# Queries' high parts, the place of a low part, and the first pair's loads in an attention with experts

## The chip, the cores and the metric

The kernel runs on one core of a Trainium2 chip, with TensorE (PE), VectorE (DVE), ScalarE (ACT), GpSimd (POOL) and SyncE (SP), which here only issues DMAs. The metric is the device time of one execution in microseconds.

## The reference

```python
q_pool = q.reshape(4, 8, 576, 2, 64).mean(axis=3)           # q, k, v: (4, 8, 1152, 64)
scores = np.matmul(q_pool, k.transpose(0, 1, 3, 2)) / 8     # 576 x 1152 per head
attn = softmax(scores)                                      # row maximum subtracted
x = np.matmul(attn, v) -> (2304, 512)
# each of the 2304 tokens goes to the expert of its largest logit (x @ w_gate, 8 experts)
x[mask_e] = gate * (np.maximum(x[mask_e] @ w1[e], 0) @ w2[e])   # 512 -> 1024 -> 512
out = ((x @ w_a) * (x @ w_b)) @ w_out                           # 512 -> 1536 -> 512
```

## The kernel before

All large products use two float16 parts of each operand: a high part, written by ScalarE, and a low part, the remainder, by VectorE (`scalar_tensor_tensor`: scaled source minus high part) or GpSimd. The work has three stages: the attention (to about 550 us), the experts over slots of 64 tokens, and the last two products.

The attention goes over 16 pairs of heads, `p` = 0 to 15, each in 21 units `u` (`n` = 21 p + u). The program's order is written by hand, and each engine executes its instructions in that order. In unit `n` the loop emits, in this order: the groups `a_units` that are due, the scores of unit `n + 1`, loads and preparation of later pairs (`load`, `prep_k`, `prep_q` and so on, at the units in the table `U`), `norm`, `turn`, `turn_low` and `logits` for the pair before, `p_low` of unit `n - 1` and the product with the values `av` of unit `n - 4`.

- `load(p)` brings raw queries (`qr`, two loads for each head) and keys (`kr`) by five DMAs on SP.
- `prep_q` adds neighbouring queries (GpSimd; VectorE for pair 0) and ScalarE writes the high part `qn[:, :, 0, :]`. `prep_q_low` copies it on VectorE to `qn[:, :, 1, :]` and writes the low part `qln`. `trans_q1` turns both by DMA transposes on SP into `qq` and `qlt`; `trans_k` does so for the keys (`kst`). `spread` copies the last tile of each.
- `a_units` are one or two PE groups of scores in high precision, into a slot of the PSUM pool `ps_a` (tile `sa`, two slots); VectorE reduces each to row maxima `mx`. `finish_max` makes a correction from them that goes through the transposition `rl` (SP) into the scores' second product. The list `a_ends` says by which unit how many groups have been emitted.
- `scores` go to two PSUM slots (`sp`); ScalarE reads each twice (`pt` in float32, `ph` in float16). `p_low` (`pl`) is GpSimd's, and `av` uses `ph` and `pl`.
- `turn(p - 1)` transposes finished outputs on PE into a slot of the same pool `sa` (tile `tp`), ScalarE writes the high part `axh`, and `turn_low` the low part `axl` on VectorE, which is the slot's last reader. Tiles 0 to 3 are turned in unit 7 and their low part comes in unit 9; tile 4 in units 10 and 11. `U["ql"]` puts `prep_q_low(p + 2)` into unit 9 as well, and ahead of `turn_low`.

```python
ps_a = ...tile_pool(name="ps_a", bufs=BA // 2, space=PSUM)      # BA = 4
U = dict(v=[12, 15], vl=[14, 19], kl1=[0, 1], ql1=1, load=12, k=[0, 2], kl=[1, 3], q=6, ql=9,
         n0=13, n1=4, nt=6, t=[7, 10], tl=[9, 11], lg=13, sx=17, g=15, lr=18, lv=1, kc=2, mg=12)
```

Ahead of the loop pair 0 is loaded and prepared at once, with PE kept busy by products of ones (`keep_warm`), the first 15 of pair 0's 27 groups of maxima follow, and `load(1)`, `load_v(0)`, `load(2)` stand on SP behind pair 0's transposes. Behind the loop the last pair's outputs are normalised, turned and routed (`scales`, `gate`, `route`), each in small steps that `aside` takes from the list `gates`.

Of the kernel before, what the change touches and what calls it, by code (L numbers as in the profile page):

```python
# [10 lines left out]
F32 = mybir.dt.float32  # L11
# [16 lines left out]
def attn_moe_kernel(  # L28
# [221 lines left out]
    def bh(p):  # L250
        return p // HP, 2 * (p % HP)

    def load(p):
        b, h = bh(p)
        s = st[p] = {}
        s["kr"] = er2.tile([128, 2, NC, D], F32, tag="kr", name=f"kr{p}")
        s["qr"] = er2.tile([128, 9, 2 * D], F32, tag="qr", name=f"qr{p}")
        for j in range(2):
            nc.sync.dma_start(
                out=s["qr"][:, 4 * j : 4 * j + 4],  # L260
                in_=q[b, h + j, 0:1024].rearrange("(i p r) d -> p i (r d)", p=128, r=2),
            )
            nc.sync.dma_start(
                out=s["qr"][64 * j : 64 * j + 64, 8],
                in_=q[b, h + j, 1024:1152].rearrange("(p r) d -> p (r d)", r=2),
            )
        nc.sync.dma_start(out=s["kr"], in_=k[b, h : h + 2].rearrange("h (p c) d -> p h c d", c=NC))
# [31 lines left out]
    def prep_q(p, eng=nc.gpsimd):  # L299
        s = st[p]  # L300
        qs = s["qs"] = er.tile([128, 9, D], F32, tag="qs", name=f"qs{p}")
        qn = s["qn"] = er2.tile([128, 9, 2, D], F16, tag="qn", name=f"qn{p}")
        eng.tensor_tensor(out=qs, in0=s["qr"][:, :, 0:D], in1=s["qr"][:, :, D:], op=ALU.add)
        nc.scalar.activation(qn[:, :, 0, :], qs, AF.Copy, scale=SC)

    def prep_q_low(p):
        qs, qn = st[p]["qs"], st[p]["qn"]
        nc.vector.tensor_copy(qn[:, :, 1, :], qn[:, :, 0, :])
        nc.vector.scalar_tensor_tensor(
            out=qlnb[p % 3][:, :, 0:D], in0=qs, scalar=SC, in1=qn[:, :, 0, :], op0=ALU.mult, op1=ALU.subtract  # L310
        )
# [15 lines left out]
    def trans_q1(p):  # L327
        s = st[p]
        qq = s["qq"] = qqb[p % 3]
        trans(qq[:, 0 : 9 * 128], s["qn"].rearrange("p t r d -> p (t r d)"))  # L330
        qlt = s["qlt"] = qltb[p % 2]
        trans(qlt[:, 0 : 9 * 128], qlnb[p % 3].rearrange("p t c -> p (t c)"))
# [546 lines left out]
    with tc.manual_schedule():  # L879
        A_0 = 3  # L880
        load(0)
# [10 lines left out]

        keep_warm(37)
        prep_q(0, nc.vector)
        for j in range(2):
            prep_k(0, j)
        prep_q_low(0)
        trans_q1(0)
        spread(0)
        for j in range(2):  # L900
            prep_k_low(0, j)
            trans_k(0, slice(j, j + 1))
        for i in range(3):
            nc.gpsimd.memset(k2b[i][64:66], MC)
        load(1)
        load_v(0)
        load(2)
# [16 lines left out]
        for j in range(2):  # L924
            prep_v(0, j)
            prep_v_low(0, j)
        keep_warm(6)

        def twos(p, ones):
# [5 lines left out]
            (NU * p - 5, 15 - A_0 + 27 * p) for p in range(3, NPAIR)  # L935
# [19 lines left out]
        def l_eng(n):  # L955
# [5 lines left out]
            v=[12, 15], vl=[14, 19], kl1=[0, 1], ql1=1, load=12, k=[0, 2], kl=[1, 3], q=6, ql=9,  # L961
# [3 lines left out]
        for n in range(NPAIR * NU):  # L965
# [10 lines left out]
            if a_due(n + 1) < a_due(n) + 2 and n + 1 < NPAIR * NU:  # L976
                scores(n + 1)
            if u == (U["lv"] if p else 5) and nxt:
                load_v(p + 1)
# [21 lines left out]
            if n in U["kl1"]:  # L1001
                prep_k_low(1, U["kl1"].index(n))
            if n == U["ql1"]:
                trans_k(1)
                prep_q_low(1)
                trans_q1(1)
# [4 lines left out]
            v_ = u if p else u - 2  # L1011
# [21 lines left out]
            if p:  # L1033
                if u == U["n1"]:
                    norm(p - 1, 1)
                if u == U["nt"]:
                    norm_tail(p - 1)
                ut, utl, ulg = [(U["t"], U["tl"], U["lg"]), ([7, 13], [9, 14], 15)][not nxt]
                if u in ut:
                    turn(p - 1, [0, 1, 2, 3] if u == ut[0] else [4])  # L1040
                if u in utl:
                    turn_low(p - 1)
                if u == (U["mg"] if nxt else 15):
                    mag_x(p - 1)
                if u == ulg:
                    logits(p - 1)
                if p % HP == HP - 1 and u == U["sx"]:
                    store_x(p // HP, 0, HP - 1)
                if p % HP == 0 and u == U["g"]:
                    gates.extend(x(p // HP - 1) for x in (scales, gate))  # L1050
# [31 lines left out]
        mag_x(NPAIR - 1)  # L1082
        turn(NPAIR - 1, [0, 1, 2, 3])
        gates.append(scales(B - 1))
        while gates:
            aside()
        split_low(0, 8)
        turn_low(NPAIR - 1)
        split_low(0, 9)
# [3 lines left out]
        gates.append(gate(B - 1))  # L1093
        while gates:
            aside()
        routing = route()
        next(routing)
        for _ in routing:
            pass
# [389 lines left out]
```

## Time and profile before

| | us |
|---|---|
| three runs: median (lowest to highest) | 1289.35 (1283.31 to 1292.65) |
| profiled execution: its own time | 1293.19 |
| its span, first to last instruction | 1291.5 |
| PE busy in the span | 1176.2 |
| mean granted clock of PE, share of full speed | 0.971 |

The span and the rows come from the profiled execution alone. A number in brackets behind a row of a timeline is the idle time of the engine just before, with what ended it. PE's clock has two levels, 1.2 and 2.4 GHz; 1.00 in a window is all of it at 2.4. A PE at the lower level counts as just as busy.

### The profile page before, as it was taken

What the parts mean: (1) busy time and instruction counts of PE and PEld (TensorE: products, weight loads), DVE (VectorE), ACT (ScalarE), POOL (GpSimd) and SP (SyncE); (2) the same over time, 40 slices, a digit from 0 to 9 for tenths busy, and PEclk for the clock granted to TensorE, in tenths of its full rate; (3) what the DMA queues carried; (4) which work ended last, traced back from release to release, by engine and by line L of the source; (5) the groups of instructions that cost most, each with busy time, mean ns of one, the idle gap of its engine ahead of it and who ended that gap; (6) DMA issues with size and microseconds to landing.
All of it is one profiled execution on the core that took longest, in us unless ns stands there. A gap on an engine that the chain in (4) does not pass through costs nothing. (4 is left out here: it accounts for less than half of the span.)

```text
span 1291.5 us, 41065 instructions
## 1 busy us (share of the span) xinstructions
PE 1176.2 (91%) x17154; PEld 819.1 (63%) x17154; DVE 790.5 (61%) x1453; ACT 649.9 (50%) x1325; POOL 538.0 (42%) x504
## 2 busy tenths in 40 slices
PE   7899999999899998579979998989999999999996
PEld 6566665666566656479868997965555555555553
DVE  5878789788877886854485547248677722222221
ACT  4578787788778778532473326225433311111110
POOL 4789888788788888613244322100000000000000
PEclk9999999999999999779999998999999999999998
DMA  6766675565555533153286227013222000000000
GB/s 174 157 118 150 149 183 146 114 147 132 112 111 141 122 76 133 48 200 127 79 319 234 88 80 279 25 37 114 77 87 95 21 1 1 25 25 25 25 21 29
DMA packets 170507, 136.45 MB, mean 106 GB/s; under 512 B 101072, under 2 KB 136400, under 8 KB 170256
## 3 DMA queue, kind: packets, MB, share of 16 engines
q1 hardware_dynamic: 167056, 122.74, 35.5%
q0 software_dynamic: 3200, 10.53, 2.5%
q8 instruction: 136, 2.23, 0.7%
q14 instruction: 115, 0.94, 0.2%
HBM read 94.96 MB, written 9.74 MB: 81 GB/s over the span
## 5 line engine op out<-in xcount | busy, mean ns | idle before, releaser
L430 POOL TENSOR_TENSOR pl<-pt,ph 128x512 f16<-128x512 f32 (+1 forms) x330 | 388.6, 1197 | 92.3 <-ACT ph L412 70.6
L361 DVE TENSOR_REDUCE mx<-sa 128x2 f32<-128x768 f32 x224 | 206.0, 923 | 78.8 <-PE sa L356 76.3
L1399 PEld LDWEIGHTS <-wc 128*128 128x128 f16 x1728 | 169.5, 98 | 124.6 <-PEq L1361 4.4
L410 ACT ACTIVATE pt<-sp 128x512 f32<-128x512 f32 (+1 forms) x336 | 197.5, 588 | 96.3 <-PE sp L403 88.6
L1399 PE MATMUL ab<-x2h,wc 128*128 128x384 f16 x1152 | 211.8, 327 | 4.3 <-DVEq L1361 4.3
L1438 POOL DMA_INDIRECT out_dram<-ob,idxo x18 | 17.7, 982 | 442.3 <-DVE ob L1437 408.9
L452 PEld LDWEIGHTS <-ph 128*128 128x128 f16 (+1 forms) x2880 | 152.3, 101 | 74.3 <-issue 33.7
L412 ACT ACTIVATE ph<-sp 128x512 f16<-128x512 f32 (+1 forms) x331 | 194.8, 589 | 0.0
L356 PE MATMUL sa<-kst,qq 128*128 128x384 f16 x480 | 158.5, 331 | 12.4 <-DVE mx L361 9.8
L452 PE MATMUL av<-vv,ph 128*128 128x65 f16 (+2 forms) x2880 | 169.3, 196 | 0.0
L356 PE MATMUL sa<-kst,qlt 128*128 128x384 f16 x480 | 158.0, 330 | 0.0
L1409 DVE TENSOR_TENSOR gf<-ab,sa 128x384 f32<-128x384 f32 x72 | 40.1, 557 | 192.5 <-PE ab L1399 192.5
L452 PE MATMUL av<-vv,pl 128*128 128x65 f16 (+1 forms) x1440 | 157.0, 195 | 0.0
L403 PE MATMUL sp<-rl,k2b 66*128 66x512 f16 (+1 forms) x576 | 136.0, 290 | 10.3 <-DMA rl<-qln 9.8
L1188 PEld LDWEIGHTS <-w2c 128*128 128x128 f16 x3840 | 126.4, 101 | 29.0 <-issue 20.8
L400 PE MATMUL sp<-qq,kst 128*128 128x512 f16 (+1 forms) x576 | 135.2, 289 | 2.0 <-ACT ph L412 1.8
L1167 PE MATMUL hp<-xh,w1c 128*128 128x64 f16 x2560 | 124.0, 193 | 4.8 <-ACTq L1314 0.9
L1167 PEld LDWEIGHTS <-w1c 128*128 128x128 f16 x3840 | 118.7, 98 | 9.7 <-DVE w1c L871 5.8
L452 PEld LDWEIGHTS <-pl 128*128 128x128 f16 (+1 forms) x1440 | 124.3, 102 | 0.0
L1167 PE MATMUL hp<-xl,w1c 128*128 128x64 f16 x1280 | 119.9, 193 | 0.0
L1188 PE MATMUL yp<-hh,w2c 128*128 128x64 f16 x2560 | 112.4, 198 | 8.0 <-issue 2.9
L1399 PE MATMUL ab<-x2l,wc 128*128 128x384 f16 x576 | 117.8, 327 | 0.0
(228 smaller groups left out, 1817.0 us busy)
## 6 DMA issues: line engine op xcount, KB each, us to landing
raw<-in_moe_w_dram SPq DMA_DIRECT2D x20, 1024.0 KB, 6.5
rbw<-in_moe_w_dram SPq DMA_DIRECT2D x20, 1024.0 KB, 7.1
kr<-in_k_dram SPq DMA_DIRECT2D x16, 576.0 KB, 5.1
vr<-in_v_dram SPq DMA_DIRECT2D x16, 576.0 KB, 5.3
qr<-in_q_dram SPq DMA_DIRECT2D x32, 256.0 KB, 3.6
cl<-in_moe_w_a_dram SPq DMA_DIRECT2D x12, 512.0 KB, 3.5
cl<-in_moe_w_b_dram SPq DMA_DIRECT2D x12, 512.0 KB, 3.5
cl<-in_moe_w_out_dram SPq DMA_DIRECT2D x12, 512.0 KB, 3.5
```

Of the source, the lines that this page charges most:

```text
L356: nc.tensor.matmul(sa[:, i, :KA], lhsT=x[:, 128 * b_ : 128 * b_ + 128], rhs=kst[:, j, ks], start=o == 0, stop=o == len(ops) - 1,)
L361: nc.vector.tensor_reduce(out=s["mx"].rearrange("p t n -> p (t n)")[:, ones[0] : ones[0] + m].rearrange("p (m o) -> p m o", o=1), in_=sa[: ...
L400: nc.tensor.matmul(sp[:, o : o + w], lhsT=s["kst"][:, j, ks], rhs=s["qq"][:, c0 : c0 + w], start=True, stop=False)
L403: nc.tensor.matmul(sp[:, o : o + w], lhsT=k2b[p % 3][:, j, ks], rhs=s["rl", j if w > 64 else 1][0:66, c0 : c0 + w], start=False, stop=True,)
L410: nc.scalar.activation(pt[:, :o], sp[:, :o], AF.Exp, scale=1.0 / (16.0 * SC * SC))
L412: nc.scalar.activation(phb[n % NPB][0][:, :o], sp[:, :o], AF.Exp, scale=1.0 / (16.0 * SC * SC))
L430: eng.tensor_tensor(out=l[:, :w], in0=pts.pop(n)[:, :w], in1=h[:, :w], op=ALU.subtract)
L452: nc.tensor.matmul(o, lhsT=a, rhs=b_, start=first, stop=False, skip_group_check=True)
L1167: nc.tensor.matmul(hp[:, j], lhsT=wc[:, t, i], rhs=g[x][:, i, w], start=first, stop=(j == 3 and i == KD - 1 and x == "xl"), skip_group_che ...
L1188: nc.tensor.matmul(y[:, d], lhsT=wc[:, t, 128 * d : 128 * d + 128], rhs=hs[s, n][x][:, j], start=first, stop=(n == 1 and len(terms) == 1 a ...
L1399: nc.tensor.matmul(ps[:, 0:TB], lhsT=w_[:, t, m, 128 * i : 128 * i + 128], rhs=x_[:, i, ts_], start=(i + j == 0), stop=(j == 2 and i == KD ...
L1409: nc.vector.tensor_tensor(out=gf, in0=pair[1], in1=sa, op=ALU.mult)
```

## The change

In the attention only:

- ScalarE writes the queries' high part to both places of `qn` in one instruction, from a source read twice; VectorE's copy goes. `prep_q`, `prep_q_low` and `trans_q1` take a range of tiles.
- `turn_low` is emitted right behind the scores, ahead of the unit's other work, instead of near its end.
- `a_ends` has the maxima from pair 3 on end one unit sooner (`NU * p - 6`).
- Pair 0's loads are split between SP's and ScalarE's queues, with pair 1's keys on ScalarE's behind head 1's queries. Pair 0's preparation goes tiles 0 to 3, head 0's keys, then tiles 4 to 8, head 1's keys, each with its transposes at once. Five products of ones fewer.
- Pair 1's low parts and transposes go from units 0 and 1 to a place ahead of the loop; `load(2)` goes behind them, on ScalarE's queue. Pair 2's preparation and pair 3's loads come two units later in pair 0 (`u - 4`).
- Behind the loop: `mag_x` and `scales` come behind `turn_low`, `scales` between steps of `gate`, and `split_low(0, 9)` behind the first part of `route`.

```diff
-    def load(p):
+    def load_q(p, j, eng=nc.sync):
+    def load_k(p, eng=nc.sync):
+    def load(p, eng=nc.sync):
...
-    def prep_q(p, eng=nc.gpsimd):
+    def prep_q(p, eng=nc.gpsimd, ts=slice(0, 9)):
...
-        nc.scalar.activation(qn[:, :, 0, :], qs, AF.Copy, scale=SC)
+        qb = qs.rearrange("p t (r d) -> p t r d", r=1).to_broadcast([128, n, 2, D])
+        nc.scalar.activation(qn, qb, AF.Copy, scale=SC)
...
-        nc.vector.tensor_copy(qn[:, :, 1, :], qn[:, :, 0, :])
...
-        load(0)
+        load_q(0, 0)
+        load_q(0, 1, nc.scalar)
+        load_k(0)
+        load_k(1, nc.scalar)
...
-        keep_warm(37)
-        prep_q(0, nc.vector)
-        for j in range(2):
+        keep_warm(32)
+
+        for j, ts in enumerate((slice(0, 4), slice(4, 9))):
+            prep_q(0, nc.vector, ts)
             prep_k(0, j)
-        prep_q_low(0)
-        trans_q1(0)
-        spread(0)
-        for j in range(2):
+            prep_q_low(0, ts)
+            trans_q1(0, ts)
             prep_k_low(0, j)
             trans_k(0, slice(j, j + 1))
+        spread(0)
...
-        load(1)
+        for j in range(2):
+            load_q(1, j)
         load_v(0)
-        load(2)
...
         for j in range(2):
+            prep_k_low(1, j)
+        prep_q_low(1)
+        load(2, nc.scalar)
+        for j in range(2):
             prep_v(0, j)
             prep_v_low(0, j)
+        trans_k(1)
+        trans_q1(1)
         keep_warm(6)
...
-            (NU * p - 5, 15 - A_0 + 27 * p) for p in range(3, NPAIR)
+            (NU * p - 6, 15 - A_0 + 27 * p) for p in range(3, NPAIR)
...
+            ut, utl, ulg = [(U["t"], U["tl"], U["lg"]), ([7, 13], [9, 14], 15)][not nxt]
+            if p and u in utl:
+                turn_low(p - 1)
             if u == (U["lv"] if p else 5) and nxt:
                 load_v(p + 1)
...
-            if n in U["kl1"]:
-                prep_k_low(1, U["kl1"].index(n))
-            if n == U["ql1"]:
-                trans_k(1)
-                prep_q_low(1)
-                trans_q1(1)
...
-            v_ = u if p else u - 2
+            v_ = u if p else u - 4
...
-                if u in utl:
-                    turn_low(p - 1)
...
         norm(NPAIR - 1, 1)
-        mag_x(NPAIR - 1)
         turn(NPAIR - 1, [0, 1, 2, 3])
-        gates.append(scales(B - 1))
-        while gates:
-            aside()
         split_low(0, 8)
         turn_low(NPAIR - 1)
-        split_low(0, 9)
+        mag_x(NPAIR - 1)
         logits(NPAIR - 1)
...
         gates.append(gate(B - 1))
+        for _ in range(3):
+            aside()
+        gates.insert(0, scales(B - 1))
         while gates:
             aside()
         routing = route()
         next(routing)
+        split_low(0, 9)
```

## Rows read from the trace of the kernel before

**Rows 1.** The page: busy us of each engine, share of the span, instructions.

```profile
PE 1176.2 (91%) x17154; PEld 819.1 (63%) x17154; DVE 790.5 (61%) x1453; ACT 649.9 (50%) x1325; POOL 538.0 (42%) x504
```

**Rows 2.** PE's waits over the span: waiter, releaser, us in total, times, longest.

```profile
PE tp L511 <- DVE axl L519: 19.2, 13, 1.8
PE sp L403 <- DMA rl<-qln: 9.8, 9, 2.9
```

**Rows 3.** Timeline of VectorE in pair 8, unit 9: start, us, operation.

```profile
298.49 0.96 DVE L361 TENSOR_REDUCE mx<-sa 128x2 f32<-128x768 f32 x1 [0.90 <-PE sa L356]
299.36 1.33 DVE L308 COPY qn<-qn 128x576 f16<-128x576 f16 x1
300.62 1.67 DVE L309 SCALAR_TENSOR_TENSOR qln<-qs,qn 128x576 f16<-128x576 f32 x1
302.23 0.67 DVE L519 SCALAR_TENSOR_TENSOR axl<-tp,axh 128x512 f16<-128x512 f32 x1
```

**Rows 4.** Timeline of PE in the same pair, units 8 to 10.

```profile
297.64 0.32 PE L356 MATMUL sa<-kst,qq 128*128 128x384 f16 x1
298.29 0.38 PE L400 MATMUL sp<-qq,kst 128*128 128x512 f16 x1
298.72 0.22 PE L452 MATMUL av<-vv,ph 128*128 128x65 f16 x2
299.09 0.38 PE L400 MATMUL sp<-qq,kst 128*128 128x512 f16 x1
302.96 0.33 PE L511 MATMUL tp<-ident,xe 128*128 128x128 f32 x1 [1.82 <-DVE axl L519]
```

**Rows 5.** Windows of 10 us: busy time (instructions) by engine, PE's granted clock, DMA.

```profile
30.00:40.00 10.00, 6.20 (x36) 3.06 (x34) 9.05 (x9) 4.70 (x10) 7.48 (x17) 0.83 0.66 122
140.00:150.00 10.00, 8.17 (x93) 5.12 (x90) 6.32 (x9) 6.03 (x13) 8.20 (x7) 0.83 0.62 135
```

**Rows 6.** Timeline of ScalarE in pair 8, unit 6.

```profile
296.59 0.71 ACT L304 ACTIVATE qn<-qs 128x576 f16<-128x576 f32 x1
```

**Rows 7.** The page's costliest groups: busy us, mean ns, idle before.

```profile
L430 POOL TENSOR_TENSOR pl<-pt,ph 128x512 f16<-128x512 f32 (+1 forms) x330 | 388.6, 1197 | 92.3 <-ACT ph L412 70.6
L361 DVE TENSOR_REDUCE mx<-sa 128x2 f32<-128x768 f32 x224 | 206.0, 923 | 78.8 <-PE sa L356 76.3
```

**Rows 8.** Timeline of PE at the start of pair 10.

```profile
350.28 0.38 PE L403 MATMUL sp<-rl,k2b 66*128 66x512 f16 x1 [1.56 <-DMA rl<-qln]
```

**Rows 9.** DMA issues of the span: operation, count, median us to landing.

```profile
rl<-qln SPq DMA_TRANSPOSE x17, 3.2
```

**Rows 10.** Timeline of SP's queue at the start.

```profile
3.08 0.59 SPq L267 DMA_DIRECT2D kr<-in_k_dram  x1
...
10.79 2.86 SPq L316 DMA_TRANSPOSE kst<-kn  x2
```

**Rows 11.** Timeline of PE's waits up to unit 2 of pair 0.

```profile
14.29 0.32 PE L356 MATMUL sa<-kst,qq 128*128 128x384 f16 x1 [2.41 <-DMA kst<-kn]
...
27.93 0.38 PE L403 MATMUL sp<-rl,k2b 66*128 66x512 f16 x1 [2.93 <-DMA rl<-qln]
...
32.20 0.32 PE L356 MATMUL sa<-kst,qq 128*128 128x384 f16 x1 [0.63 <-DVE mx L361]
...
36.62 0.48 PE L356 MATMUL sa<-kst,qq 128*128 128x384 f16 x1 [3.17 <-DVE mx L361]
```

**Rows 12.** Timeline of ScalarE ahead of the loop.

```profile
21.45 0.68 ACT L291 ACTIVATE kn<-kr 128x576 f16<-128x576 f32 x1 [8.35 <-DMA kr<-in_k_dram]
...
25.46 1.25 ACT L277 ACTIVATE vv<-vr 128x576 f16<-128x576 f32 x2
```

**Rows 13.** Timeline of VectorE in unit 1 of pair 0.

```profile
32.83 1.27 DVE L308 COPY qn<-qn 128x576 f16<-128x576 f16 x1
34.02 1.67 DVE L309 SCALAR_TENSOR_TENSOR qln<-qs,qn 128x576 f16<-128x576 f32 x1
```

**Rows 14.** Timeline of VectorE behind the last pair.

```profile
541.66 0.20 DVE L596 TENSOR_REDUCE tot<-rp 128x8 f32<-128x40 f32 x1 [0.43 <-PE rp L590]
```

More of the change, by code (lines that the diff above doesn't have):

```diff
@@ L251, in bh @@
         return p // HP, 2 * (p % HP)
-    def load(p):
+    def load_q(p, j, eng=nc.sync):
         b, h = bh(p)
-        s = st[p] = {}
+        if "qr" not in st.setdefault(p, {}):
+            st[p]["qr"] = er2.tile([128, 9, 2 * D], F32, tag="qr", name=f"qr{p}")
+        qr = st[p]["qr"]
+        eng.dma_start(
+            out=qr[:, 4 * j : 4 * j + 4], in_=q[b, h + j, 0:1024].rearrange("(i p r) d -> p i (r d)", p=128, r=2)
+        )
+        eng.dma_start(
+            out=qr[64 * j : 64 * j + 64, 8], in_=q[b, h + j, 1024:1152].rearrange("(p r) d -> p (r d)", r=2)
+        )
+    def load_k(p, eng=nc.sync):
+        b, h = bh(p)
+        s = st.setdefault(p, {})
         s["kr"] = er2.tile([128, 2, NC, D], F32, tag="kr", name=f"kr{p}")
-        s["qr"] = er2.tile([128, 9, 2 * D], F32, tag="qr", name=f"qr{p}")
+        eng.dma_start(out=s["kr"], in_=k[b, h : h + 2].rearrange("h (p c) d -> p h c d", c=NC))
+    def load(p, eng=nc.sync):
         for j in range(2):
[L259 to L267, printed above, removed]
+            load_q(p, j, eng)
+        load_k(p, eng)
     def load_v(p):
@@ L297, in prep_k_low, with prep_q_low @@
         )
-    def prep_q(p, eng=nc.gpsimd):
+    def prep_q(p, eng=nc.gpsimd, ts=slice(0, 9)):
         s = st[p]
-        qs = s["qs"] = er.tile([128, 9, D], F32, tag="qs", name=f"qs{p}")
-        qn = s["qn"] = er2.tile([128, 9, 2, D], F16, tag="qn", name=f"qn{p}")
-        eng.tensor_tensor(out=qs, in0=s["qr"][:, :, 0:D], in1=s["qr"][:, :, D:], op=ALU.add)
-        nc.scalar.activation(qn[:, :, 0, :], qs, AF.Copy, scale=SC)
-    def prep_q_low(p):
-        qs, qn = st[p]["qs"], st[p]["qn"]
-        nc.vector.tensor_copy(qn[:, :, 1, :], qn[:, :, 0, :])
+        if "qs" not in s:
+            s["qs"] = er.tile([128, 9, D], F32, tag="qs", name=f"qs{p}")
+            s["qn"] = er2.tile([128, 9, 2, D], F16, tag="qn", name=f"qn{p}")
+        qs, qn = s["qs"][:, ts], s["qn"][:, ts]
+        n = qs.shape[1]
+        eng.tensor_tensor(out=qs, in0=s["qr"][:, ts, 0:D], in1=s["qr"][:, ts, D:], op=ALU.add)
+        qb = qs.rearrange("p t (r d) -> p t r d", r=1).to_broadcast([128, n, 2, D])
+        nc.scalar.activation(qn, qb, AF.Copy, scale=SC)
+    def prep_q_low(p, ts=slice(0, 9)):
+        qs, qn = st[p]["qs"][:, ts], st[p]["qn"][:, ts]
         nc.vector.scalar_tensor_tensor(
-            out=qlnb[p % 3][:, :, 0:D], in0=qs, scalar=SC, in1=qn[:, :, 0, :], op0=ALU.mult, op1=ALU.subtract
+            out=qlnb[p % 3][:, ts, 0:D], in0=qs, scalar=SC, in1=qn[:, :, 0, :], op0=ALU.mult, op1=ALU.subtract
         )
@@ L325, in copy_k, with trans_q1 @@
         nc.scalar.copy(k2b[p % 3][0:64, i // 2, w], st[p]["kst"][0:64, i // 2, w])
-    def trans_q1(p):
+    def trans_q1(p, ts=slice(0, 9)):
         s = st[p]
+        c = slice(128 * ts.start, 128 * ts.stop)
         qq = s["qq"] = qqb[p % 3]
-        trans(qq[:, 0 : 9 * 128], s["qn"].rearrange("p t r d -> p (t r d)"))
+        trans(qq[:, c], s["qn"][:, ts].rearrange("p t r d -> p (t r d)"))
         qlt = s["qlt"] = qltb[p % 2]
-        trans(qlt[:, 0 : 9 * 128], qlnb[p % 3].rearrange("p t c -> p (t c)"))
+        trans(qlt[:, c], qlnb[p % 3][:, ts].rearrange("p t c -> p (t c)"))
     def spread(p):
@@ L960, in attn_moe_kernel @@
         U = dict(
-            v=[12, 15], vl=[14, 19], kl1=[0, 1], ql1=1, load=12, k=[0, 2], kl=[1, 3], q=6, ql=9,
+            v=[12, 15], vl=[14, 19], load=12, k=[0, 2], kl=[1, 3], q=6, ql=9,
             n0=13, n1=4, nt=6, t=[7, 10], tl=[9, 11], lg=13, sx=17, g=15, lr=18, lv=1, kc=2, mg=12,
@@ L1037, in attn_moe_kernel @@
                     norm_tail(p - 1)
-                ut, utl, ulg = [(U["t"], U["tl"], U["lg"]), ([7, 13], [9, 14], 15)][not nxt]
                 if u in ut:
                     turn(p - 1, [0, 1, 2, 3] if u == ut[0] else [4])
-                if u in utl:
-                    turn_low(p - 1)
                 if u == (U["mg"] if nxt else 15):
```

## The prediction

> **What bounds the kernel now.** First the page: TensorE (PE) is busy 91% of the span, VectorE 61, ScalarE 50, GpSimd 42 [rows 1]. More than half of the time, from about 560 us on (the experts and the last stage), runs code that the diff doesn't touch, so only what PE loses ahead of that can be won. The second view is PE's waits, summed by releaser: 19.2 us in 13 waits for VectorE's low part of a turned output and 9.8 us in 9 waits for the transposed maxima `rl` [rows 2]. Third, one steady pair on PE and VectorE. A `turn` fills a slot of the two-slot pool `sa`, and `turn_low` empties it. In unit 9 VectorE does a reduce, then `prep_q_low`'s copy (1.33 us) and subtraction (1.67 us), and only then the low part, from 302.23 to 302.90 [rows 3]; PE's next transposition, which wants the slot, starts at 302.96 after 1.82 us of waiting [rows 4]. Eight of the 13 waits are 1.81 to 1.83 us long; the others (two early pairs, three pairs with a gate in them) are 0.56 to 1.54. Pair 14, in which there is no `prep_q_low`, has none, which speaks for the queue on VectorE as the cause.
>
> The clock is the fourth view. It falls to 1.2 GHz for about 3.4 us behind four of those eight waits; a 10 us window around one shows 0.83 granted [rows 5]. Each fall costs half of 3.4 us, 1.7 us. No wait of up to 1.56 us has a fall behind it.
>
> **The change, part by part.** The sum is made against the profiled execution, 1293.2 us, of which the span is 1291.5; the median of the runs is 1289.35, 3.8 us lower.
>
> *The low part moved ahead, the copy gone.* In the changed order unit 9 of a normal pair has a score group for the maxima (`a_units`) of its own, because the maxima's plan ends a unit earlier (-6 for -5). I lay rows end to end, 0 being that group's start. On PE a group takes 0.65 us (297.64 to 298.29), scores 0.43, outputs 0.37 [rows 4]: PE comes to unit 10's transposition at 0.65 + 0.43 + 0.37 + 0.43 = 1.88. VectorE's reduce starts when the group has landed, about 0.85, takes 0.87 before the next operation can start, then the low part 0.67 [rows 3]: 2.39. A wait of 0.5 us is left of 1.82. Behind it VectorE has the subtraction (1.61 from start to start), unit 11's reduce (0.87) and the second low part (0.28), so until about 5.1; PE comes to unit 12's group, which needs that slot, at about 4.4: a new wait of 0.7. Together 1.2 us, so 0.6 us are won in each of eight pairs, about 1 us in each of the three gate pairs, where VectorE is fullest and loses 1.33 us of work, and 0.3 in each of the two early ones: 4.8 + 3 + 0.6 = **8.4 us**. The bounds: 3 us, if only the gate pairs win, and 19, the whole row [rows 2].
>
> *The clock.* Waits of 0.5 and 0.7 us lie under all those that had no fall behind them, so the four falls go: **6.8 us** (0 to 6.8).
>
> *ScalarE's double write.* A write of 576 elements takes 0.71 us and holds the engine 0.57 [rows 6]; twice the elements hold it up to 0.57 longer, 16 times. ScalarE is busy half the span [rows 1]; in unit 6 the next exponentials start that much later, and scores two units on need their slot; at PE's pace [rows 4] they have about 1 us to spare. I take 0; if that cover is gone, 0.57 x 15 = 8.6 us. GpSimd's part (1.2 us a unit, 388.6 us in all [rows 7]) then fills about 26 of the 29 us of a pair; four units lie between its operation and its reader, so it costs nothing yet.
>
> *Maxima one unit sooner.* From pair 3 on six `rl` waits, 0.30 to 1.56 us (the longest but for the first: [rows 8]), sum to 5.4. A transposition lands 3.2 us after its issue [rows 9]; one unit is 0.8 to 1.45 us. I take **4.5 us** (0 to 5.4); the new neighbours are the five loads issued on SP in unit 12, and if they delay the landing nothing is won.
>
> *First loads and transposes.* The key load of pair 0 is SP's fifth issue, at 3.08 us [rows 10]; with head 1's queries on ScalarE's queue it is the third, 1.2 us sooner. The Trainium skill ("DMA: Bandwidth & Descriptors", Issuing engines are not separate DMA queues) says that a second issuing engine saves only the sequencer's time, as all queues share the same 16 DMA engines; by it this would give at most the 1.2 us, and pair 1's keys, now in the same stretch, could take it back. The rows of this case don't show ScalarE's queue at all. The first key transposition now waits in SP's queue behind two long ones until 10.79, and PE starts at 14.29 [rows 10, 11]; behind two half ones it can go at about 10. So PE's first group comes some 0.8 us sooner (between 0.5 later and 1.5 sooner); it is counted below, where ScalarE decides what arrives. The five warm-up products fewer (1.45 us) lie inside a wait of 2.41 us; if that wait grew and the clock fell, 1.7 us.
>
> *Maxima of pair 0 and pair 2's loads.* `rl` lands only at 27.93 [rows 11], with the loads of pairs 1 and 2 in front of it; without pair 2's, and issued 0.8 us sooner, at some 21.5, it would land after the usual 3.2 us [rows 9], at about 24.7. But the five loads now stand in ScalarE's own queue ahead of `prep_v` and of the first exponential. ScalarE reaches them at about 23.6 (it no longer waits until 21.45 for pair 1's keys [rows 12], but its query part still waits for GpSimd's sum, at about 21.4). At SP's 0.59 an issue [rows 10] that is 2.9 us, then 1.25 for the values [rows 12]: the first exponential at about 27.7 instead of 28.3, just behind the landing of `rl`. I take **0.7 us**. If an issue holds ScalarE for next to nothing it is 3; if each takes as long as one of SP's transposes, 1.43 [rows 10], it is a loss of 4.
>
> *Pair 1's low parts ahead of the loop.* In units 0 and 1 VectorE now does two key parts, the copy (1.27) and the subtraction (1.67) [rows 13], and PE waits 0.63 and 3.17 us for maxima behind them [rows 11], the second with a fall of the clock (0.83 in that window [rows 5]): 3.8 + 1.7 = 5.5. Ahead of the loop they lie beside ScalarE's issues and values, which hide them; uncovered they would cost their 5 us. Pair 2's own steps go two units later: its transposes are issued in unit 13 and first read in unit 17, some 5.8 us on, against about 6.2 (subtraction 1.6, the first transposition's issue 1.4, the second's landing 3.2): 0.5 lost. **5.0 us** (2 to 5.5).
>
> *The end of the attention.* `mag_x` and `scales` go behind the last low part, and one weight part behind the index. VectorE then waits some 0.75 us for ScalarE's turned part, where the wait of 0.43 for the ranks' products goes [rows 14]; PE's next work hangs on the end of that chain. **0.3 us lost** (1 won to 1.5 lost).
>
> The sum: 8.4 + 6.8 + 4.5 + 0.7 + 5.0 - 0.3 = 25.1 us. From 1293.2 that gives 1268.1, from the median 1264.3. I say 1265.
>
> **The rivals.**
> VectorE is late next, all over: the waits for the low part come back as waits for maxima (3 us won), two of four falls stay (3.4), `rl` gives 3, the start 4: 13.4 us, about 1278. For it: VectorE is at nine tenths in gate pairs; against it: it sits idle 76 us ahead of its reduces, waiting for PE's groups [rows 7].
> The low part doesn't set PE's wait, because the releaser is inferred: neither waits nor falls go, 25.1 - 15.2 = 9.9 won, about 1281. Pair 14 speaks against it.
> Slower: the two short waits per pair, so close together, drop the clock in all 13 pairs. Nine falls more cost 15.3 us, the waits' sum stays, and ScalarE's longer write adds up to 8.6 with PE slow to refill; the rest gives 9.9 and no falls go: 14 us lost, about 1305. It decides where falls come in more than about nine pairs. The Trainium skill ("TensorE: Matmul & The Clock Gate", A second HAM failure mode: psum-queue depth-cycling) describes just that, frequent short idles between groups that swing the clock; the rows here show no fall behind a wait under 1.8 us, so I hold it unlikely.
> ScalarE's queue is the bound at the start: 4 lost there in place of 0.7 won, and half of 8.6 in the pairs, 9 in all, 16 won: about 1275.
>
> **How the numbers follow.** Forecast 0.60, VectorE late 0.14, low part not the cause 0.08, ScalarE 0.12, slower 0.06. The forecast's own range goes from 1249, with all terms at their better ends (19 + 6.8 + 5.4 + 3 + 5.5 + 1 = 40.7 off the median), to 1275, where the low part gives 3 and two falls stay. Until no more than 2 in 10 is left out it reaches to the second and third rival: 1249 to 1283. A median of three runs of this kernel, which spread over 9 us, can hardly tell less than 1%, 12.9 us; faster by more is all under 1276.5: the forecast, ScalarE's case for the most part, and a third of the first rival, 0.77; slower by more than 1% is part of the clock's case, 0.05; within 1% the rest, 0.18.
>
> **What would show it.** PE's waits for the low part under 8 us in all; none of 1.8; the 10 us windows of pairs 3 to 13 at 1.00 granted; `rl` waits from pair 3 on under 1 us together; no 3.17 us wait at 33 to 37 us and no fall there; ScalarE's loads of pair 2 as issues of some 0.6 us ahead of the first exponential; sixteen query writes of about 1.25 us. The prediction is wrong if a pair still takes 30 us or more between its `rl` issues (28.3 plus waits is what the rows allow), or if new waits on ScalarE or GpSimd stand on PE.

## The result and the profile after

The changed kernel takes 1272.02 us (median of four runs, 1269.38 to 1272.47); the kernel before, in the same rounds, 1288.86. The ratio is 0.9868 [0.983, 0.9907]: faster by 1.3%. The forecast was 1265 in a range of 1249 to 1283. The profiled execution took 1272.47, its span 1270.8, 20.7 us under the span before; PE's mean granted clock is 0.972 (0.971 before).

PE's waits in the changed kernel, over the span (waiter, releaser, us in total, times, longest):

```profile
PE sa L368 <- DVE mx L373: 10.9, 19, 1.7
PE sp L415 <- DMA rl<-qln: 7.8, 6, 4.4
PE sp L412 <- ACT ph L424: 6.3, 10, 3.0
PE sa L368 <- DMA kst<-kn: 4.1, 1, 4.1
```

Against [rows 2] the 19.2 us for the low part are gone without a rest. But three of the lines hold one long wait each (4.4, 3.0, 4.1); the longest of the same kind before were 2.9, 0.9 and 2.4.

To see where they lie, take one operation that both kernels have, the normalisation of four output tiles on VectorE, and read its start in pair 1 (unit 4) and in the last pair. First before, then after:

```profile
77.18 0.42 DVE L484 TENSOR_TENSOR xe<-av,rec 128x256 f32<-128x256 f32 x1
...
535.16 0.42 DVE L484 TENSOR_TENSOR xe<-av,rec 128x256 f32<-128x256 f32 x1
```

```profile
82.42 0.42 DVE L496 TENSOR_TENSOR xe<-av,rec 128x256 f32<-128x256 f32 x1
...
517.76 0.42 DVE L496 TENSOR_TENSOR xe<-av,rec 128x256 f32<-128x256 f32 x1
```

The start loses 5.2 us (77.18 to 82.42). The stretch between the two marks shrinks from 457.98 to 435.34: 22.6 won. From the last mark to the first expert product it is 24.00 before (ends 559.16) and 23.45 after (541.21): 0.5 won. From there to the end 732.3 before and 729.6 after, code that the change doesn't touch: 2.7. Together 22.6 + 0.5 + 2.7 - 5.2 = 20.6, but for rounding the 20.7 of the spans. Below, "the start" and "the pairs" mean these two stretches.

**The pairs.** VectorE in pair 8 from unit 9 on, in the changed kernel:

```profile
294.37 0.96 DVE L373 TENSOR_REDUCE mx<-sa 128x2 f32<-128x768 f32 x1 [1.73 <-PE sa L368]
295.25 0.68 DVE L531 SCALAR_TENSOR_TENSOR axl<-tp,axh 128x512 f16<-128x512 f32 x1
295.84 1.36 DVE L320 SCALAR_TENSOR_TENSOR qln<-qs,qn 128x576 f16<-128x576 f32 x1
297.14 0.94 DVE L373 TENSOR_REDUCE mx<-sa 128x2 f32<-128x768 f32 x1
```

PE beside it:

```profile
293.52 0.33 PE L368 MATMUL sa<-kst,qq 128*128 128x384 f16 x1
...
295.35 0.38 PE L412 MATMUL sp<-qq,kst 128*128 128x512 f16 x1 [0.22 <-ACT ph L424]
...
295.79 0.27 PE L523 MATMUL tp<-ident,xe 128*128 128x128 f32 x1
...
298.13 0.32 PE L368 MATMUL sa<-kst,qq 128*128 128x384 f16 x1 [0.26 <-DVE mx L373]
```

Compare [rows 3, 4]: the low part follows its reduce at once, and the transposition at 295.79 has no wait of its own where there were 1.82 us. It even starts 0.14 us before the low part ends (295.25 + 0.68 = 295.93), so it no longer waits for that at all. What is left of the pair's waits is 0.22 for `ph` and 0.26 for the maxima. The windows of 10 us from 90 to 500 us all show 1.00 granted; before, four falls lay there.

**The start.** Windows of 10 us in the changed kernel (columns as in [rows 5]):

```profile
10.00:20.00 10.00, 5.87 (x34) 4.55 (x32) 5.34 (x9) 4.37 (x9) 0.00 (x0) 0.83 0.72 148
...
30.00:40.00 10.00, 8.87 (x51) 4.61 (x51) 4.79 (x5) 6.40 (x12) 5.75 (x8) 0.83 0.95 193
...
80.00:90.00 10.00, 9.76 (x107) 6.41 (x106) 6.99 (x13) 8.49 (x16) 8.63 (x8) 0.84 0.48 90
```

Three falls, and ahead of each a long wait of PE (timeline of the changed kernel):

```profile
14.36 0.32 PE L368 MATMUL sa<-kst,qq 128*128 128x384 f16 x1 [4.13 <-DMA kst<-kn]
...
31.13 0.38 PE L415 MATMUL sp<-rl,k2b 66*128 66x512 f16 x1 [4.40 <-DMA rl<-qln]
...
78.32 0.38 PE L412 MATMUL sp<-qq,kst 128*128 128x512 f16 x1 [2.95 <-ACT ph L424]
```

ScalarE and its queue (ACTq rows are issues) tell what stands behind the three:

```profile
1.94 0.81 ACTq L269 DMA_DIRECT2D kr<-in_k_dram  x1
...
9.48 0.68 ACT L298 ACTIVATE kn<-kr 128x576 f16<-128x576 f32 x1 [4.22 <-DMA kr<-in_k_dram]
...
23.97 1.16 ACT L316 ACTIVATE qn<-qs 128x1152 f16<-128x1152 f32 x1 [4.91 <-POOL qs L314]
23.98 0.37 ACTq L258 DMA_DIRECT2D qr<-in_q_dram  x1
...
31.54 0.60 ACT L422 ACTIVATE pt<-sp 128x512 f32<-128x512 f32 x1 [3.38 <-PE sp L415]
...
76.62 0.68 ACT L298 ACTIVATE kn<-kr 128x576 f16<-128x576 f32 x1 [3.62 <-DMA kr<-in_k_dram]
```

SP's queue:

```profile
1.90 0.58 SPq L269 DMA_DIRECT2D kr<-in_k_dram  x1
...
24.51 1.44 SPq L327 DMA_TRANSPOSE rl<-qln  x1
...
66.75 1.57 SPq L258 DMA_DIRECT2D qr<-in_q_dram  x1
```

Pair 0's keys are issued at 1.90 instead of 3.08 [rows 10], yet ScalarE has them at 9.48; before it had them at 8.06:

```profile
8.06 1.26 ACT L291 ACTIVATE kn<-kr 128x576 f16<-128x576 f32 x2 [1.04 <-DMA kr<-in_k_dram]
```

The first maxima `rl` are issued at 24.51 and PE gets them at 31.13, 6.6 us later (3.2 is usual [rows 9]; before, with the loads of pairs 1 and 2 in front, it was 22.25 to 27.93, 5.7). And in pair 1 ScalarE waits 3.62 us for pair 3's keys, with exponentials queued behind, so PE finds no free slot for scores. Three hypotheses: pair 1's keys delay pair 0's; pair 2's loads delay `rl`; pair 3's loads, two units later, are too late.

### The profile page after: what moved, and what is told of

It reads as the page before. It is cut to its first block, busy times and chain, and to the rows that moved or that the text cites. A ratio compares the mean times of both kernels' runs of the same rounds, so it can differ in the third digit from the quotient of the medians.

```text
span 1270.8 us, 41031 instructions
## 1 busy us (share of the span) xinstructions
PE 1169.6 (92%) x17144; PEld 817.7 (64%) x17144; DVE 782.9 (62%) x1439; ACT 655.5 (52%) x1326; POOL 531.4 (42%) x504
## 5 line engine op out<-in xcount | busy, mean ns | idle before, releaser
L464 PEld LDWEIGHTS <-ph 128*128 128x128 f16 (+1 forms) x2880 | 149.2, 100 | 68.2 <-issue 25.5
L368 PE MATMUL sa<-kst,qq 128*128 128x384 f16 x480 | 157.5, 328 | 17.2 <-DVE mx L373 10.9
L1203 PEld LDWEIGHTS <-w2c 128*128 128x128 f16 x3840 | 125.9, 101 | 29.1 <-issue 23.7
```

The costliest lines, as they stand in the source:

```text
L368: nc.tensor.matmul(sa[:, i, :KA], lhsT=x[:, 128 * b_ : 128 * b_ + 128], rhs=kst[:, j, ks], start=o == 0, stop=o == len(ops) - 1,)
L464: nc.tensor.matmul(o, lhsT=a, rhs=b_, start=first, stop=False, skip_group_check=True)
L1203: nc.tensor.matmul(y[:, d], lhsT=wc[:, t, 128 * d : 128 * d + 128], rhs=hs[s, n][x][:, j], start=first, stop=(n == 1 and len(terms) == 1 a ...
```

## The experiments

Marks and waits are from the profiled executions, one for each kernel; times are medians. How far one mark can be trusted: the kernel before, e3 and e5 run the same code up to the first mark and reach it at 77.18, 77.02 and 79.08. The first four kernels are the kernel before with parts of the change in the pairs alone.

**e1_pairs**: the three edits in the pairs, the old start and the old end.

```diff
-        nc.scalar.activation(qn[:, :, 0, :], qs, AF.Copy, scale=SC)
+        qb = qs.rearrange("p t (r d) -> p t r d", r=1).to_broadcast([128, 9, 2, D])
+        nc.scalar.activation(qn, qb, AF.Copy, scale=SC)
...
-        nc.vector.tensor_copy(qn[:, :, 1, :], qn[:, :, 0, :])
...
-            (NU * p - 5, 15 - A_0 + 27 * p) for p in range(3, NPAIR)
+            (NU * p - 6, 15 - A_0 + 27 * p) for p in range(3, NPAIR)
...
+            if p and u in utl:
+                turn_low(p - 1)
...
-                if u in utl:
-                    turn_low(p - 1)
```

> Kernel before with the three edits inside the pairs alone: double write by ScalarE, low part early, maxima one unit sooner; its start and its end are those of before. Theory A (the gain comes from the pairs, the changed start loses): PE's waits for the low part fall from 19.2 us to under 2, no fall of the clock behind them, about 22 us won against before, so about 5 us better than the whole change: 1266. Theory B (the start is needed for the pairs to run well, as part of the loss at the start is only work moved there): no more than 17 us won, 1272 or more.

1270.72 us against 1288.39, ratio 0.9835 [0.9778, 0.9892]. The pairs take 435.2 us, as in the changed kernel (435.3); the start ends at 78.80, 3.6 us sooner than in the changed kernel. So these three edits hold the whole gain.

**e3_low_first**: only the low part's place.

```diff
...
+            if p and u in utl:
+                turn_low(p - 1)
             if u == (U["lv"] if p else 5) and nxt:
...
-                if u in utl:
-                    turn_low(p - 1)
```

> Kernel before with the low part moved ahead of the unit's other work and nothing else; the copy stays. Theory A (the place in VectorE's queue makes the wait): the waits for the low part go nearly whole, 19.2 us to under 3, with the falls of the clock behind them; new waits for maxima behind copy and subtraction of up to 0.7 us a pair take some back; 12 to 20 us won. Rival (the copy's 1.3 us of VectorE's time is what is too much): the wait goes elsewhere, under 6 us won.

1272.36, ratio 0.9879 [0.9828, 0.993]. The pairs take 440.1 (77.02 to 517.13): 17.9 won. Waits on PE:

```profile
PE sa L356 <- DVE mx L361: 19.4, 24, 3.2
PE sp L403 <- DMA rl<-qln: 10.1, 11, 2.7
```

The low part's waits are gone. In their place the subtraction and the copy, still on VectorE, keep the next reduce waiting, 0.80 us in a normal pair (the line was 9.8 us before); one early pair has 2.22, at 86.51. No window from 80 to 500 us shows a fall.

**e4_write_twice**: only the double write in place of the copy.

```diff
-        nc.scalar.activation(qn[:, :, 0, :], qs, AF.Copy, scale=SC)
+        qb = qs.rearrange("p t (r d) -> p t r d", r=1).to_broadcast([128, 9, 2, D])
+        nc.scalar.activation(qn, qb, AF.Copy, scale=SC)
...
-        nc.vector.tensor_copy(qn[:, :, 1, :], qn[:, :, 0, :])
```

> Kernel before with the copy gone and ScalarE writing the high part twice, and nothing else; the low part stays behind the subtraction. Theory A (place): the low part comes 1.3 us sooner, so eight waits of 1.8 us become 0.5 and the waits for the low part sum to about 6 us instead of 19.2; short waits have no fall of the clock behind them: 12 to 18 us won, so that place and copy each alone give most of it and don't add up. Rival (ScalarE's longer write holds the exponentials up): waits of PE for ScalarE of 0.5 us a pair, under 8 us won.

1269.30, ratio 0.9829 [0.9782, 0.9875]. The pairs take 434.25 (76.92 to 511.17): 23.7 won, as much as with all three edits.

```profile
PE tp L511 <- DVE axl L519: 4.9, 8, 0.7
...
PE sp L400 <- ACT ph L412: 2.2, 6, 0.9
```

Seven waits of 0.65 and one of 0.30 remain, with no fall from 90 to 500 us. The line for ScalarE's `ph` was 1.8 before: the double write costs at most 0.4 us in all.

**e5_six**: only the maxima a unit sooner.

```diff
-            (NU * p - 5, 15 - A_0 + 27 * p) for p in range(3, NPAIR)
+            (NU * p - 6, 15 - A_0 + 27 * p) for p in range(3, NPAIR)
```

> Kernel before with the maxima ending one unit sooner and nothing else. Theory A: the rl waits from pair 3 on go (5.4 us), but unit 9 gets a score group of its own, whose reduce stands ahead of copy, subtraction and low part, so the waits for the low part grow to about 2.4 to 3 us a pair, with more falls of the clock: between 5 us won and 15 us lost. Rival (maxima and low part don't meet): 5 us won and the 19.2 us unchanged.

1289.01, ratio 1.0002 [0.9979, 1.0025]: nothing. The pairs take 454.6, 3.4 less.

```profile
PE sa L356 <- DVE axl L519: 19.1, 11, 2.5
PE sp L403 <- DMA rl<-qln: 4.4, 2, 3.9
...
PE tp L511 <- DVE axl L519: 2.8, 2, 1.6
```

From pair 3 on nothing waits for `rl` any more, but unit 9 now holds a group of its own, and the wait for the low part stands in front of a later group that wants the slot, up to 2.5 us long, with the falls still there (windows between 170 and 410 us with 0.83 to 0.96).

**e6_start**: the changed start with the pairs and the end of before.

```diff
-        qb = qs.rearrange("p t (r d) -> p t r d", r=1).to_broadcast([128, n, 2, D])
-        nc.scalar.activation(qn, qb, AF.Copy, scale=SC)
+        nc.scalar.activation(qn[:, :, 0, :], qs, AF.Copy, scale=SC)
...
+        nc.vector.tensor_copy(qn[:, :, 1, :], qn[:, :, 0, :])
...
-            (NU * p - 6, 15 - A_0 + 27 * p) for p in range(3, NPAIR)
+            (NU * p - 5, 15 - A_0 + 27 * p) for p in range(3, NPAIR)
```

(relative to the changed kernel; `turn_low` and the end go back likewise)

> Changed start alone (loads, transposes, pair 0's and pair 1's order), with the pairs and the end of before: copy back, low part late, maxima at their old unit. Theory A (the start loses): PE comes to pair 1's unit 4 about 5 us later than before (82 against 77 us), and the whole is 2 to 6 us slower than before. Rival (the start's loss seen in the changed kernel comes from how its parts meet the new pairs): same as before or faster.

1301.43 against 1292.23, ratio 1.0061 [1.004, 1.0083]: the start alone makes the kernel slower. Its mark comes at 81.31 (4.1 us late), and the pairs take 459.0, with 20.1 us of low-part waits and five falls.

The next three are the changed kernel with one step of its start undone, one for each hypothesis.

**e7_two_units**: pair 3's loads and pair 2's preparation at their old unit.

```diff
-            v_ = u if p else u - 4
+            v_ = u if p else u - 2
```

> Changed kernel with pair 0's shift back at two units (u - 2), so pair 3's loads go out in unit 14 again and pair 2's preparation begins in unit 2. Theory A (in the changed kernel ScalarE waits 3.6 us for pair 3's keys in unit 0 of pair 1, PE 2.95 us behind it, with a fall of the clock, because those loads go out two units later, behind rl on SP): that wait goes, 4 to 5 us won against the changed kernel. Rival (ScalarE waits because the DMA engines are full, whenever the loads go out): the wait stays, or pair 2's keys are now waited for in unit 2; under 2 us won.

1267.80, ratio 0.9818 [0.9795, 0.9841]. The waits at 14 and 31 us stay (4.09, 4.34); the 2.95 in pair 1 and its fall are gone, and the start ends at 76.23, 6.2 us sooner than in the changed kernel.

**e8_keys_back**: pair 1's keys back on SP, behind pair 1's queries.

```diff
-        load_k(1, nc.scalar)
...
         for j in range(2):
             load_q(1, j)
+        load_k(1)
```

> Changed kernel with pair 1's keys on SP again, behind pair 1's queries. Theory A (they share the DMA engines with pair 0's keys): pair 0's first key part starts on ScalarE about 1 to 1.5 us sooner than 9.48, PE's first group at about 13 us instead of 14.36, its wait falls from 4.1 to under 3 us, and the clock's fall behind it goes, 1.7 us: about 3 us won at the first maxima; but pair 1's keys now hold up ScalarE's copies as before. Rival (pair 0's keys are late for another reason, the early transposes): no change there.

1270.20, ratio 0.9827 [0.9805, 0.9848]. ScalarE and PE:

```profile
6.90 0.68 ACT L298 ACTIVATE kn<-kr 128x576 f16<-128x576 f32 x1 [1.55 <-DMA kr<-in_k_dram]
...
71.28 0.68 ACT L298 ACTIVATE kn<-kr 128x576 f16<-128x576 f32 x1 [4.76 <-DMA kr<-in_k_dram]
```

```profile
11.70 0.32 PE L368 MATMUL sa<-kst,qq 128*128 128x384 f16 x1 [0.28 <-DMA kst<-kn]
...
24.63 0.38 PE L415 MATMUL sp<-rl,k2b 66*128 66x512 f16 x1 [2.21 <-DMA rl<-qln]
...
72.99 0.58 PE L412 MATMUL sp<-qq,kst 128*128 128x512 f16 x1 [4.09 <-ACT ph L424]
```

Pair 0's keys, issued at 1.90 as in the changed kernel, are used at 6.90 instead of 9.48, and PE starts at 11.70 instead of 14.36, with no fall up to 70 us. The same mark in pair 0 (unit 13) comes at 53.03 instead of 59.16. Then pair 1 gives part of it back: PE comes there sooner, pair 3's keys do not, the wait is 4.09 and a fall follows; the start ends at 77.34. The other profiles agree: PE's first group comes between 14.12 and 14.65, with a fall in 10 to 20 us, in the four kernels with pair 1's keys on ScalarE's queue (the changed one, e6, e7, e9), and between 11.70 and 12.01, without one, in the five that have them on SP's (e8, e10 to e13).

**e9_loads_behind_rl**: pair 2's loads on SP, right behind the first `rl`.

```diff
         finish_max(0, [0])
+        load(2)
...
-        load(2, nc.scalar)
```

> Changed kernel with pair 2's five loads on SP right behind the first rl transposition, instead of on ScalarE's queue. Theory A (rl lands 6.6 us after its issue because pair 2's loads share the DMA engines with it): it lands about 3.3 us after, the wait of 4.4 us falls to 1 or 2, the fall of the clock behind it goes: 3 to 5 us won. Rival (rl is late for pair 1's key transposes or pair 1's loads): the wait stays at 4 us.

1269.82, ratio 0.9836 [0.9812, 0.986]. SP issues `rl` at 24.58, and PE, without a fall in 30 to 40 us, has

```profile
27.89 0.38 PE L415 MATMUL sp<-rl,k2b 66*128 66x512 f16 x1 [1.64 <-DMA rl<-qln]
...
37.60 0.34 PE L368 MATMUL sa<-kst,qq 128*128 128x384 f16 x1 [1.11 <-DMA qq<-qn]
```

So `rl` takes 3.3 us from its issue. The edit also moves pair 1's key transposes on SP from 27.15 to 28.99, behind the landing, so e9 by itself doesn't part the loads from them. In e10 (below) these transposes are issued at 24.43, when PE has `rl` (24.39, issued at 19.77), and it still took 4.6 us, with loads of pairs 1 and 2 about it: loads alone make `rl` later than the usual 3.2. The wait of 1.11, and one of 1.05 behind it, are for pair 1's transposes, which now stand in SP's queue behind the five loads; the start ends at 77.24.

**e10_both_back**: e7 and e8 together (both diffs above).

> Changed kernel with pair 1's keys on SP again and pair 0's shift back at two units. Theory A (two separate costs at the start, each with a fall of the clock): pair 0's unit 13 at about 53 us as with the keys alone, pair 1's unit 4 at about 72 instead of 82.4 in the changed kernel and 77.2 before, no wait for ScalarE over 1.5 us and no fall of the clock up to pair 13: 9 to 11 us won against the changed kernel, about 1261. Rival (what is won at the start is lost again to the loads of pairs 2 and 3, which now come sooner): pair 1's unit 4 at 76 or later, 1266 or more.

1262.63 against 1289.33, ratio 0.9787 [0.9751, 0.9822]. The start ends at 71.63, the pairs take 434.6. PE's waits at the start:

```profile
11.80 0.32 PE L368 MATMUL sa<-kst,qq 128*128 128x384 f16 x1 [0.99 <-DMA kst<-kn]
...
24.39 0.38 PE L415 MATMUL sp<-rl,k2b 66*128 66x512 f16 x1 [1.87 <-DMA rl<-qln]
...
28.54 0.38 PE L412 MATMUL sp<-qq,kst 128*128 128x512 f16 x1 [2.03 <-ACT ph L424]
```

One fall is left, in 30 to 40 us (0.84), behind the wait for ScalarE's `ph`. ScalarE ahead of it:

```profile
21.78 0.68 ACT L298 ACTIVATE kn<-kr 128x576 f16<-128x576 f32 x1 [7.54 <-DMA kr<-in_k_dram]
...
24.08 1.16 ACT L316 ACTIVATE qn<-qs 128x1152 f16<-128x1152 f32 x1
...
27.43 0.57 ACT L422 ACTIVATE pt<-sp 128x512 f32<-128x512 f32 x1
```

It waits for pair 1's keys, then works without a gap, and the exponentials come last.

**e11_all_three**: e10 with e9's edit too.

> As the run before, and pair 2's loads on SP right behind the first rl transposition instead of on ScalarE's queue. Theory A: ScalarE's wait of 1.4 us and rl's of 2.2 ahead of the loop shrink; 1 to 2 us more won than without. Rival: pair 1's transposes queue behind those loads on SP, and PE waits for them 1 to 2 us in units 5 to 7, so nothing is won.

1261.03, ratio 0.9785 [0.9752, 0.9819]; the start ends at 71.37. Nothing that could be told from e10; the wait for `ph` is still there (2.02 us), so pair 2's issues on ScalarE's queue were not its cause.

**e12_write_only**: e10's start and end; in the pairs only the double write.

```diff
-            (NU * p - 6, 15 - A_0 + 27 * p) for p in range(3, NPAIR)
+            (NU * p - 5, 15 - A_0 + 27 * p) for p in range(3, NPAIR)
...
-            if p and u in utl:
-                turn_low(p - 1)
...
+                if u in utl:
+                    turn_low(p - 1)
```

(relative to e10)

> As the first of these three, but in the pairs only ScalarE's double write is left: low part at its old place behind the subtraction, maxima at their old unit. Theory A (each of the edits in the pairs takes the same wait away, so beside the double write the other two add nothing): from pair 1's unit 4 to the last pair's end 434 us, as with all three (435), and the same time within 3 us. Rival (with a faster start the short waits for the low part, 4.9 us in all, come back as falls of the clock): 5 us or more slower than with all three.

1263.47, ratio 0.9801 [0.9769, 0.9833]; the pairs take 437.1, 2.5 us more than in e10.

PE waits 10.9 us for `rl` in all and 5.7 for the low part (eight waits of 0.65, one of 0.45), and the clock falls nowhere between 90 and 500 us. Whether the other two edits are worth anything with the copy gone is not shown: here all three are 2.5 us better by the marks, with the old start they were 0.9 worse (435.2 in e1, 434.25 in e4), and the times can't tell.

**e13_keys_first**: e10, and pair 1's keys loaded ahead of its queries.

```diff
+        load_k(1)
         for j in range(2):
             load_q(1, j)
-        load_k(1)
         load_v(0)
```

> The kernel with both steps of the start undone (pair 1's keys on SP, pair 3's loads at their old unit), and pair 1's key load now ahead of pair 1's query loads on SP instead of behind them. In the kernel without this edit ScalarE waits 7.5 us for pair 1's keys, until 21.8 us, and then works without a gap until 27.4, so that the first exponential starts 3 us behind the first maxima, PE waits 2.03 us at 28.5 and the clock falls in 30 to 40 us. If ScalarE's order behind the late keys is the cause: its key part starts at about 19.5, the first exponential at about 25.5, PE's wait for ph at the start falls under 0.8 us, the fall in 30 to 40 us goes, the mark in pair 1 comes at about 68.5 to 70.5 instead of 71.6, and the time is about 1260. If the queries, now 0.6 us later, and GpSimd's sum of them set ScalarE's end instead: ScalarE's query part starts at 24 or later as it did, the first exponential stays at 27 or later, and mark and time stay where they were (71.6 and 1262.6). If the keys, now issued ahead, take the DMA engines from the first maxima or from pair 0's last transposes: PE's waits for kst or rl grow by 1 us or more and the mark comes later than 72.

1265.75 against 1290.68, ratio 0.9806 [0.9778, 0.9834]: not better than e10. ScalarE:

```profile
19.22 0.68 ACT L298 ACTIVATE kn<-kr 128x576 f16<-128x576 f32 x1 [4.87 <-DMA kr<-in_k_dram]
...
23.16 1.16 ACT L316 ACTIVATE qn<-qs 128x1152 f16<-128x1152 f32 x1 [1.54 <-POOL qs L314]
...
26.04 1.26 ACT L284 ACTIVATE vv<-vr 128x576 f16<-128x576 f32 x2 [0.58 <-issue]
27.20 0.58 ACT L422 ACTIVATE pt<-sp 128x512 f32<-128x512 f32 x1
```

The keys come 2.6 us sooner, and then ScalarE waits for GpSimd's sum of the queries, which now land later: the first exponential gains 0.23 us, PE's wait is 2.27, the fall stays, the start ends at 71.50. The second of the expected cases.

## Why the prediction was right, and where it was not

The direction and the range held, and 1265 was 7 us too low: the pairs gave 2.9 us more than forecast and the start, forecast at 5.7 won, lost 5.2. The start's two terms were bounded at 2 lost to 8.5 won together, so they fell outside. That the sum came as near as it did is in part luck: the misses have opposite signs, and 2.7 us of what the profiles won lies in code that the change doesn't touch. The sums themselves come out; the rivals' times are counted from midway between the profiled execution and the median, the forecast from the median.

**The pairs** (low part 8.4, clock 6.8, maxima 4.5: 19.7 forecast, 22.6 measured). By waits between the marks, summed over all releasers: 36.7 us before, 18.8 after. With four falls of 1.7 that makes 17.9 + 6.8 = 24.7, less some 0.4 that the changed kernel still pays, behind its first mark, of the fall that began at 79 us. The remaining 1.7 us are not accounted for. So waits and falls did go as forecast. The maxima's term was right in size: waits for `rl` from pair 3 on fell from 5.4 to 1.3 us, if not under the 1 that was named. The low part's term was mis-sized: the waits other than for `rl` fell by 13.8, where 8.4 was forecast.

Its working had a step wrong. It let unit 10's transposition wait 0.5 us for the low part, and unit 12's group 0.7 us for the second low part. VectorE went as laid out: counted from the group's start, the low part ended at 2.41 (295.93 less 293.52; forecast 2.39). PE came to the transposition at 2.27, not at 1.88 (its outputs took 0.5 us instead of 0.37, and 0.22 for `ph` came in between), and did not wait for the low part. Unit 12's group started at 298.13, just behind a reduce (297.14 + 0.94 = 298.08) and before the second low part's end at 298.27. The group that unit 9 now has makes the two slots change roles: the transposition takes the one that this group's reduce has emptied, and the low part's goes to a later group, which comes 0.33 us after its end (296.26). e5, which has the same group and the low part still late, shows it openly: its transposition in pair 8 starts at 302.41, while the low part runs from 304.18 to 304.85, and the next group waits for that until 304.90. So the forecast's two waits stood in front of the wrong operations. In the three gate pairs the rest is larger, one wait of 1.30 and two of about 0.3.

**The edits are not a sum.** The prediction put the copy and the low part's place into one term and did not see that either would do. The double write alone wins 23.7 us between the marks, the early low part alone 17.9, and they win the same thing: either brings PE's wait in a normal pair from 1.82 down to between 0.65 and 0.81, and no fall was seen behind that. -6 alone wins 3.4 and moves the low-part wait to another tile.

**ScalarE's double write** at 0: right. It takes 1.16 us; the wait for `ph` grew by 0.4 us in e4, and between the marks from 1.8 to 3.3 with all three edits (after, e1).

**First loads and transposes** (0.8 sooner within the 0.7, with "if that wait grew and the clock fell, 1.7"): a step that failed. It said that pair 1's keys could take the 1.2 us back and bounded PE's first group at 0.5 us later. The group came at 14.36 instead of 14.29, within that bound; but the sum took 0.8 us sooner and nothing for a fall. What the sharing costs is 9.48 - 6.90 = 2.6 us, shown by e8, in which the keys come at just the 1.2 us sooner that the issue order promises (8.06 to 6.90). The Trainium skill ("DMA: Bandwidth & Descriptors", Issuing engines are not separate DMA queues) says that DMAs of different issuing engines run interleaved on the same 16 DMA engines; these 2.6 us agree. PE's first wait grew from 2.41 to 4.13, and the clock fell. That growth is not the keys' alone: the group came 0.07 later, while the products of ones, five fewer, took 9.08 us instead of 10.72. They were taken out because they lay inside a wait, and the wait grew by as much. (In e6 and e9, with the same loads, the ones took 10.23 and 10.10, the waits were 3.27 and 2.88, and the clock fell too.) The early keys of e8 end wait and fall together; the changed loads with all 37 products were not tried.

**Maxima of pair 0 and pair 2's loads** (0.7 won): the wrong price was looked for. What was costed was ScalarE's time for the issues. They took 0.37 to 0.62 us each, and those that met earlier activations ran beside them (the write at 23.97, an issue at 23.98); only the values, behind them in the queue, were held, 0.63 us in the changed kernel and 0.58 in e13. The cost lay in the transfers: they met `rl`, which landed 6.6 us after its issue, no sooner than the 5.7 of before. With the loads behind `rl` (e9) it was 3.3. And `rl` was issued at 24.51, not at the 21.5 that was laid out, as its maxima began later than that and came from a PE at the lower clock.

**Pair 1's low parts ahead of the loop** (5.0): the waits of 0.63 and 3.17 [rows 11] are gone, as forecast, with no wait in their place in those units. But pair 2's preparation "two units later: 0.5 lost" counted only its transposes. Pair 3's loads go with the same variable; issued from 66.75 on (57.03 before), behind `rl` on SP, their keys reach ScalarE at 76.62, and the exponentials stand behind: 2.95 us and a fall. And pair 2's subtraction, moved by the same variable, now runs on VectorE at 57.46, ahead of pair 1's maxima:

```profile
60.50 0.32 PE L368 MATMUL sa<-kst,qq 128*128 128x384 f16 x1 [1.74 <-DVE mx L373]
```

With the old unit (e7) that wait is 0.43. Both waits and the fall make up most of the 6.2 us of e7. A moved step's loads have a reader, and on a queue in order that reader blocks whatever comes next.

With both mistakes taken back (e10) the start ends 5.6 us sooner than before, where 0.7 and 5.0 were forecast for these steps, though one fall is left in it.

**The end of the attention**: 0.5 won where 0.3 was lost; within its bounds.

**The signs that were named.** No wait for the low part and none of 1.8 is left, and the windows of pairs 3 to 13 are at 1.00. But two of the signs of being wrong came too. A pair takes 30 us or more between its `rl` issues in the three gate pairs (30.2 to 31.4 us; 28.0 to 29.9 in the other pairs from 3 on). And a new wait on ScalarE, 2.95 us at 78.32, stands on PE. The fall that was to go from 33 to 37 us is back, behind another wait, 4.40 for `rl`.

**The rivals.** VectorE late next: not in the changed kernel (10.9 us of waits for maxima, 9.8 before), but in e3 (19.4), as long as the copy is still there. Low part not the cause: refuted by e3. Falls in all pairs: none in the pairs of the changed kernel; the Trainium skill's depth-cycling ("TensorE: Matmul & The Clock Gate", A second HAM failure mode: psum-queue depth-cycling) was not seen behind waits of 0.2 to 0.8 us, pair after pair (the changed kernel, e3, e4). ScalarE the bound at the start: in the changed kernel ScalarE itself was waiting for the maxima and for keys; in e10 and e13 it is the bound, at 2.0 to 2.3 us and a fall.

What stays open: how to take the last wait at the start away. e11 and e13 show that neither pair 2's issues nor the keys' arrival alone sets it; keys and queries of pair 1 are both needed ahead of the first exponential by ScalarE's order. An order with the exponentials first wasn't tried.

## What to carry to other kernels

Cost a moved load by when its bytes land and who reads them next in order, not by its issue; a load put on a second queue beside an urgent one took 2.6 us from that one here. Warm-up work that lies inside a wait is not free to take out: the wait grows by as much. Edits that relieve the same wait don't add: try each alone first, and price the rest against what is left. Where a wait is long enough that the clock falls behind it, halving it can be worth as much as removing it (e4).

## What was not expected of the hardware

VectorE's subtractions of 576 elements took different times with GpSimd idle and busy. Pair 1's key parts, in e10 with GpSimd idle (its sum ended at 21.49):

```profile
22.49 0.76 DVE L302 SCALAR_TENSOR_TENSOR kn<-kr,kn 128x576 f16<-128x576 f32 x1 [1.44 <-ACT kn L298]
```

and in e13, where GpSimd's sum ran from 21.43 to 23.12:

```profile
21.12 2.62 DVE L302 SCALAR_TENSOR_TENSOR kn<-kr,kn 128x576 f16<-128x576 f32 x2
```

1.31 us each, for the most part beside it, 0.76 alone. It isn't always VectorE that loses: in the kernel before a key part took 0.83 us at 32.07, with GpSimd at work from 30.63 to 33.93, and there GpSimd's `p_low` took 1.67 us instead of 1.15. The queries' subtraction, which the change doesn't alter, took 1557 ns on average (16 times) in the kernel before, 1353 with the copy gone (e4) and 1381 with the low part moved (e3); what it met on GpSimd there was not looked into.

From the last mark to the end, code that is the same in both took 751.0 us in e3 and 758.5 in e4. So several us of one execution's time are not its edit's. Marks leave these out, but with the same code a mark was still 2 us apart (77.02 and 79.08).

No fall of the clock stood from 90 to 500 us behind a wait of up to 1.56 us. Falls came behind waits of 1.8 us and more, but not behind each: in the kernel before, four of the eight waits of 1.8 had one behind them, and the 2.93 at 27.93 had none; nor had the 2.21 in e8 and the 2.22 in e3. A wait's length alone doesn't decide.
